# Side stages' matmuls ranked first in the planner, and three operands moved to other byte offsets

## The chip, the cores and the metric

One core of one Trainium2 chip runs the kernel. TensorE (PE for its matmuls, PEld for its weight loads), VectorE (DVE), ScalarE (ACT) and GpSimd (POOL) work side by side; transfers are issued from the SP queue. The metric is the device time in microseconds of one execution. The kernel before took 2572.21 us, the median of three runs (2569.39 to 2573.22). Outside the profile's span lie some 2 us of each execution.

## The reference

For x of shape 8 x 3008 x 256 the reference takes the real FFT along the sequence, multiplies every frequency by a complex 256 x 256 matrix and adds a complex bias, shrinks real and imaginary part towards zero by 0.01, and transforms back. The result, as 24064 rows of 256, goes through a feed-forward layer.

```python
X = np.fft.rfft(x, axis=1)
Yr = Xr @ w_r - Xi @ w_i + b_r
Yi = Xr @ w_i + Xi @ w_r + b_i
Yr, Yi = soft_threshold(Yr, 0.01), soft_threshold(Yi, 0.01)
y = np.fft.irfft(Yr + 1j * Yi, n=3008, axis=1)
h = y @ w_in                      # 256 -> 2048
out = (h * np.clip(h + 3, 0, 6) / 6) @ w_out    # 2048 -> 256
```

## The kernel before

The feed-forward layer is the bulk. It is cut into 47 chunks of 512 rows and 8 bands of the hidden width, 376 units. A unit goes through four phases of `w_in` matmuls (`phase_a` to `phase_d`, a Strassen form with seven block products), a gate on ScalarE and VectorE (`gate`), and four steps of `w_out` matmuls (`down`). Every operand here is a pair of fp32r numbers, high and low, and a product is three matmuls: low x high, high x low, high x high (`product`, line 137; `down`, line 651). All of these matmuls have 256 columns. Stationary operands are `w_in` and `w_out`, moving ones `yb` and `gs`.

The Fourier transforms are the side stages, one batch after the other, and all but the first batch run between the feed-forward units:

- `stage1` (line 268): 47-point transforms over blocks of 120 rows. For batches 2 to 7, and most of batch 1, it splits the data into `xs` (high, low) and calls `product`, three matmuls of 512 columns (256 for the last block), with the constant `f47` stationary and `xs` moving.
- `middle` (line 366) for each of 12 groups of two frequencies: `s2` (line 390), four fp32 matmuls of 128 columns on the loaded tile `bt`; `s3`, 18 matmuls of 256 columns with the weights `w_r`, `w_m`, `w_i` moving; `s4`, which splits `zt` into `z`; `s5` (line 465), a `product` of three matmuls of 512 columns with the constant `g64` stationary and `z` moving.
- `segment` (line 485): 47-point transforms back, seven segments in a batch; for each half `dh` four fp32 matmuls of 120 columns (two of 96 in the last segment) on the loaded tile `qt`, whose results go into the chunks `raw` of the feed-forward layer. `qt` has one buffer, `bt` two.

An fp32 matmul stands in the trace as two records, an fp32r one as one.

All side stages put their results into PSUM tiles called `ps_a`, of which there are two (`room`); in the stages of batch 0 some go to `pb`. Their tiles are handed out in program order.

The order on each engine is made by a planner when the kernel is built: it plays the program against durations that it assumes, and on every engine it takes, of the instructions whose inputs it believes ready, the one of the best rank. The rank is the position in the program, unless an instruction stands under `tc.high_priority()`: that one comes ahead of all others. Before the change this holds for the copies and additions that empty the feed-forward PSUM tiles (`kept`, `added`), and for no matmul. The program puts the pieces of the side stages into slots between the units' phases (`lay`, `slots`, `fill`). On the chip each engine keeps the planner's order, and an instruction whose input is not there holds up all behind it.

SBUF is laid out by hand, through the order in which tiles are made and through small filler tiles. Tiles with the same `tag` share a place. With the bytes of each tile added up, the starts modulo 256 are: `w_in` and `w_out` 160, `X` 160, `z` and `xs` 160, `f47` 192 (high) and 128 (low), `g64` 96, `yb`, `gs`, `bt`, `qt` and the weights `w_r`, `w_m`, `w_i` 96. A filler `gap` of 192 bytes behind `X` turns 160 into 96.

```python
home = ("a", "h", "z", "h", "xs", "h", "X")[q % 7] if b == 0 else ("a", "ot", "ot")[q % 3] if b == 1 and whole else "a"
a = space([P, 2 * D], F32, "a", home)[:rows, :w]
if home == "X":
    space([P, 48], F32, "gap")
```

In batch 0 `stage1` borrows places for its results `a` by these tags; the order in which the tags first occur is the order of the places.

Of the kernel before, what the change touches and what calls it, by code (L numbers as in the profile page):

```python
# [23 lines left out]
NK = N2 // 2 + 1  # L24
# [76 lines left out]
def spectral_ffn(ctx: ExitStack, tc: tile.TileContext, x, w_r, w_i, bias, w_in, w_out, f47, f64, g64, sgn, out):  # L101
# [31 lines left out]
    def product(ps, terms, start=True, stop=True, more=False):  # L133

        todo = [p for (ah, al), (bh, bl) in terms for p in ((al, bh), (ah, bl), (ah, bh))]
        for n, (a, b) in enumerate(todo):
            nc.tensor.matmul(  # L137
                out=ps,
                lhsT=a,
                rhs=b,  # L140
                start=start and n == 0,
                stop=stop and n == len(todo) - 1,
                skip_group_check=more,
            )
# [122 lines left out]
    split(*f47_s)  # L267


    scr1, scr2, stores = {}, {}, []  # L270

    def stage1(b):
        scr1[b] = dram.tile([2, N1, NK, D], F32, name="scr1")
        sets = SEGS[-1:] + SEGS[:-1]
        xins = {}

        def load(i):
            n1, n = sets[i]
            rows, w = (R47, 2 * D) if n == 2 * J else (n * NK, D)
            if b == 0:  # L280
                xins[i] = spare[i]
            elif b == 1 and i < 4:
                if i % 2 == 0:
                    xins[i], xins[i + 1] = twin([P, 2, 2 * D], F32, "xin", "gs")
            else:
                xins[i] = space([P, 2, 2 * D], F32, "xin")
            at = n1 // J * 2 * D
            src = x[b, :rows, at : at + 2 * w].rearrange("p (s c) -> p s c", s=2)
            nc.sync.dma_start(out=xins[i][:rows, :, :w], in_=src)
            return rows, w  # L290

        shapes = [load(i) for i in range((len(sets), 4, 1)[min(b, 2)])]
        for i, (n1, n) in enumerate(sets):
            rows, w = shapes[i]
            xin = xins.pop(i)
            plus, minus = xin[:rows, 0, :w], xin[:rows, 1, :w]
            whole = b == 0 or b == 1 and i < 4
            e = space([P, 2 * D], F32, "e", "r" if whole else "e")[:rows, :w]
            on = nc.vector if whole else nc.gpsimd
            on.tensor_tensor(out=e, in0=plus, in1=minus, op=ALU.add)  # L300
            on.tensor_tensor(out=plus, in0=plus, in1=minus, op=ALU.subtract)
            for c, src in enumerate((e, plus)):
                q = 2 * i + c
                if whole:
                    ps = room(c == 1)
                    turns = f47_s[2][:rows, c * R47 : c * R47 + rows]
                    nc.tensor.matmul(out=ps[:rows, :w], lhsT=turns, rhs=src, start=True, stop=True)
                else:
                    xs = [t[:rows, :w] for t in twin([P, 2 * D], F32R, "xs")]
                    split(*xs, src, nc.gpsimd)  # L310
                    yield
                    ps = room()
                    product(ps[:rows, :w], [([t[:rows, c * R47 : c * R47 + rows] for t in f47_s[:2]], xs)])
                home = ("a", "h", "z", "h", "xs", "h", "X")[q % 7] if b == 0 else ("a", "ot", "ot")[q % 3] if b == 1 and whole else "a"
                a = space([P, 2 * D], F32, "a", home)[:rows, :w]
                if home == "X":
                    space([P, 48], F32, "gap")
                nc.scalar.copy(out=a, in_=ps[:rows, :w])
                dst = scr1[b][c, n1 : n1 + n].rearrange("(g j) k d -> (j k) g d", g=w // D)
                stores.append(nc.sync.dma_start(out=dst, in_=a.rearrange("p (g d) -> p g d", d=D)))  # L320
                if c and i + 1 < len(sets) and i + 1 >= len(shapes) and not whole:
                    shapes.append(load(i + 1))
                yield
            if whole and i + 1 == len(shapes) and i + 1 < len(sets):
                shapes.append(load(i + 1))

    bias_s = const.tile([P, 2 * D], F32, name="bias")
    sgn_s = const.tile([P, NK], F32, name="sgn")
    w_m = [const.tile([P, 2 * D], F32R, name="w_m_" + t) for t in ("hi", "lo")]
    w_four = []  # L330

# [18 lines left out]
        yield  # L350

    run(stage1(0))
    with tc.issue_after(stores[-1].ins):
        r, k = [loaded(w, P, 2 * D, n, t) for w, n, t in ((w_r, "w_r", spare[7]), (w_i, "w_i", spare[8]))]
        nc.sync.dma_start(out=bias_s, in_=bias)
        g64_t = loaded(g64, P, P, "g64")
        nc.sync.dma_start(out=sgn_s, in_=sgn)
        const.tile([P, 16], F32, name="last")
    w_four += [twin([P, 2 * D], F32R, "w", tag) for tag in ("T", "qt")]
# [11 lines left out]
    def middle(b):  # L371
# [16 lines left out]
        def s2(g):  # L388
            data, f = bt.pop(g)
            ps = room(b == 0)  # L390
            psv = ps.rearrange("p (h r k c) -> p h r k c", h=2, r=2, k=2)
            for u in range(2):
                for dh in range(2):
                    nc.tensor.matmul(  # L394
                        out=psv[:, dh, :, u, :],
                        lhsT=data[:, u, dh * P : (dh + 1) * P],
                        rhs=f[:, u, :],
                        start=True,
                        stop=True,
                    )  # L400
            if g + 2 < NG:
                load(g + 2)
            pv = ps.rearrange("p (h r c) -> p h r c", h=2, r=2)
            hi, lo = twin([P, 2, 3, P], F32R, "X", tag(g, "X", "gs", "gs"))
            if b:
                xi = space([P, 2, P], F32, "xi")
                nc.scalar.copy(out=xi, in_=pv[:, :, 1])
            split(hi[:, :, :2], lo[:, :, :2], pv)
            if b:
                nc.vector.tensor_tensor(out=xi, in0=pv[:, :, 0], in1=xi, op=ALU.add)  # L410
                split(hi[:, :, 2], lo[:, :, 2], xi)
            xs[g] = (hi, lo)
# [52 lines left out]
        def s5(g):  # L465
            ps = room(b == 0)
            flat = lambda t: t.rearrange("p k d -> p (k d)")
            if b:
                product(ps, [(g64_s, [flat(t) for t in zs.pop(g)])])
            else:  # L470
                nc.tensor.matmul(out=ps, lhsT=g64_t[2], rhs=flat(zs.pop(g)), start=True, stop=True)
            pt = space([P, 2, D], F32, "pt", tag(g, "pt", "ot", "ot"))
            nc.scalar.copy(out=pt, in_=ps.rearrange("p (k d) -> p k d", d=D))
            nc.sync.dma_start(out=dst[:, 2 * g : 2 * g + 2, :], in_=pt)
# [20 lines left out]
    def segment(b, k, tag="qt", aside=None):  # L495
# [22 lines left out]

        for dh in range(2):
            ps = room(bool(aside) and dh == 1)  # L520
            for cs in range(2):
                for g in range(gr):
                    nc.tensor.matmul(  # L523
                        out=ps[:, cs * w + g * rows : cs * w + (g + 1) * rows],
                        lhsT=qt[:rows, cs, g, dh * P : (dh + 1) * P],
                        rhs=f47_s[2][:rows, cs * R47 : cs * R47 + rows],
                        start=True,
                        stop=True,
                    )
            odd = space([P, 2 * R47], F32, "odd", aside or "xi")[:, :w]  # L530
            nc.scalar.copy(out=odd, in_=ps[:, w : 2 * w])
            for c, q, lo, hi in places(0, w):
                nc.vector.tensor_tensor(out=raw[c][:, dh, q : q + hi - lo], in0=ps[:, lo:hi], in1=odd[:, lo:hi], op=ALU.add)

            some = lambda a: a.rearrange("p (n q) -> p n q", q=NK)[:, :, 1:]
            m = NK - 1
            for c, q, lo, hi in places(w, n * m):
                while lo < hi:
                    row, col = divmod(lo, m)
                    if col == 0 and hi - lo >= m:  # L540
                        r1, c1 = hi // m, m
                    else:
                        r1, c1 = row + 1, min(m, col + hi - lo)
                    size = (r1 - row) * (c1 - col)
                    nc.vector.tensor_tensor(
                        out=raw[c][:, dh, q : q + size].rearrange("p (n q) -> p n q", n=r1 - row),
                        in0=some(ps[:, :w])[:, row:r1, col:c1],
                        in1=some(odd)[:, row:r1, col:c1],
                        op=ALU.subtract,
                    )  # L550
                    lo, q = lo + size, q + size
            yield
# [260 lines left out]
```

## Time and profile before

| | |
|---|---|
| median of 3 runs | 2572.21 us |
| the profiled execution itself | 2572.28 us |
| its span, first to last instruction | 2570.1 us |
| PE busy | 2509.0 us, 98% of the span, 20910 records |
| PEld busy | 2449.8 us, 95% |
| DVE busy | 1969.8 us, 77% |
| ACT busy | 1823.2 us, 71% |
| POOL busy | 773.6 us, 30% |
| chain that ended last, PE's share | 89% |

A matmul's record lasts longer than the time until the next one starts, since matmuls are pipelined. So the busy time of PE says only that it is never empty; its pace is read from the starts. In the timeline view neighbours of one line and tile are merged into one row with their count, and the start of the next row less the start of this one, over the count, is the pace. The view by form gives the mean length of a record, which grows with the pace.

### The profile page before, as it was taken

The page shows a single profiled execution, that of the slowest core. Times are in us where ns is not written, and L with a number is a line of the kernel's source. Part 1 is how long each engine was busy: PE and PEld are TensorE (multiplying, and loading weights), DVE is VectorE, ACT ScalarE, POOL GpSimd, SP SyncE. Part 2 cuts the span into 40 slices and gives each one's busy share as a digit, 9 for nine tenths or more (in the row PEclk, how much of TensorE's full clock was granted, in tenths as well). Part 3 has the DMA queues.
Part 4 walks back from the last instruction along what each step waited for, and adds up shares of the span by engine and source line. Part 5 has one row for each costly group of instructions (what it writes and reads, how often), then busy time and mean ns, then how long its engine had stood idle before and what let it go on. Part 6 is the DMA issues. An engine that isn't in the chain of part 4 may idle for free.

```text
span 2570.1 us, 53411 instructions
## 1 busy us (share of the span) xinstructions
PE 2509.0 (98%) x20910; PEld 2449.8 (95%) x20910; DVE 1969.8 (77%) x3189; ACT 1823.2 (71%) x3584; POOL 773.6 (30%) x738
## 2 busy tenths in 40 slices
PE   6789999999999999999999999999999999999999
PEld 4579999999999999999999999999999999999998
DVE  7778878877787777778777777877778777767766
ACT  6477777777777777777777677767776777766676
POOL 3353442333233332333313343234321221121310
PEclk8889999999999999999999999999999999999999
DMA  8633432332133222232223222222222121110000
GB/s 245 193 114 104 131 97 83 90 91 71 58 94 87 65 71 71 80 91 72 76 73 89 66 78 84 75 78 81 71 74 60 52 66 51 37 37 21 12 18 17
DMA packets 150115, 200.54 MB, mean 78 GB/s; under 512 B 16847, under 2 KB 103943, under 8 KB 149863
## 3 DMA queue, kind: packets, MB, share of 16 engines
q1 hardware_dynamic: 149863, 197.13, 26.6%
q8 instruction: 164, 2.69, 0.5%
q14 instruction: 88, 0.72, 0.1%
HBM read 97.45 MB, written 74.97 MB: 67 GB/s over the span
## 4 chain that ended last, share of the span: by engine, by line
PE 89%; DVE 4%; DMA 3%; ACT 2%; issue 1%; SPq 1%; POOL 0%; ACTq 0%; DVEq 0%; POOLq 0%
PE po L651 38%; PE pb L137 19%; PE ps_a L137 11%; PE pc L137 9%; PE pd L137 5%; PE ps_a L523 3%; PE ps_a L394 3%; ACT gs L130 1%; DVE r L628 1%; DMA scr<-a 1%; ACT r L626 1%; DMA zt<-tc 1%; DMA x_lo<-in_x 0%; DMA bt<-scr 0%; DVE h L590 0%
## 5 line engine op out<-in xcount | busy, mean ns | idle before, releaser
L651 PE MATMUL po<-gs,w_out_hi 128*128 128x256 f32 x6016 | 1029.4, 277 | 0.0
L651 PEld LDWEIGHTS po<-gs,w_out_hi 128*128 128x128 f32 x6016 | 843.0, 188 | 1.6
L628 DVE SCALAR_TENSOR_TENSOR r<-r,h 128x1024 f32<-128x1024 f32 x376 | 479.9, 1276 | 270.0 <-ACT r L626 268.7
L651 PE MATMUL po<-gs,w_out_lo 128*128 128x256 f32 x3008 | 605.6, 279 | 2.2 <-ACT gs L130 1.1
L626 ACT ACTIVATE r<-h,three 128x1024 f32<-128x1024 f32 x376 | 434.5, 1156 | 217.3 <-DVE h L590 215.9
L137 PE MATMUL pb<-yb,w_in_hi 128*128 128x256 f32 x3008 | 570.7, 278 | 1.1 <-DVE yb L131 1.1
L131 DVE TENSOR_TENSOR gs<-r,gs 128x1024 fp32r<-128x1024 f32 x376 | 483.3, 1285 | 100.1 <-ACT gs L130 97.4
L130 ACT CAST gs<-r 128x1024 fp32r<-128x1024 f32 x376 | 395.3, 1051 | 110.7 <-DVE r L628 108.0
L651 PEld LDWEIGHTS po<-gs,w_out_lo 128*128 128x128 f32 x3008 | 461.1, 188 | 8.3 <-ACT gs L130 6.1
L137 PEld LDWEIGHTS pb<-yb,w_in_hi 128*128 128x128 f32 x3008 | 458.3, 189 | 4.6 <-DVE yb L131 1.3
L131 POOL TENSOR_TENSOR yb<-T,yb 128x256 fp32r<-128x256 f32 x184 | 172.2, 938 | 875.2 <-ACT yb L130 859.6
L137 PE MATMUL pb<-yb,w_in_lo 128*128 128x256 f32 x1504 | 427.7, 287 | 2.6 <-ACT yb L130 1.2
L590 DVE TENSOR_TENSOR h<-pc,u 128x256 f32<-128x256 f32 x752 | 314.9, 419 | 101.2 <-PE pc L137 93.0
L585 ACT COPY u<-pb 128x256 f32<-128x256 f32 x752 | 278.9, 373 | 110.4 <-PE pb L137 101.7
L137 PE MATMUL pc<-yb,w_in_hi 128*128 128x256 f32 x1504 | 296.2, 278 | 0.6 <-DVE yb L131 0.6
L137 PEld LDWEIGHTS pb<-yb,w_in_lo 128*128 128x128 f32 x1504 | 282.9, 189 | 7.7 <-ACT yb L130 1.4
L137 PEld LDWEIGHTS pc<-yb,w_in_hi 128*128 128x128 f32 x1504 | 228.9, 189 | 1.7 <-DVE yb L131 0.9
L137 PE MATMUL pc<-yb,w_in_lo 128*128 128x256 f32 x752 | 212.9, 283 | 1.3 <-DVE h L590 1.2
L585 ACT COPY p<-pb 128x256 f32<-128x256 f32 x376 | 139.3, 371 | 53.8 <-PE pb L137 51.3
L619 ACT COPY h<-pb 128x256 f32<-128x256 f32 x376 | 140.9, 375 | 39.2 <-PE pb L137 37.7
L590 DVE TENSOR_TENSOR h<-pd,p 128x256 f32<-128x256 f32 x376 | 156.8, 417 | 9.4 <-ACT p L585 6.8
L131 POOL TENSOR_TENSOR xs<-xin,xs 120x512 fp32r<-120x512 f32 (+1 forms) x45 | 58.7, 1304 | 321.1 <-ACT xs L130 307.8
(139 smaller groups left out, 3989.0 us busy)
## 6 DMA issues: line engine op xcount, KB each, us to landing
bt<-scr SPq DMA_DIRECT2D x96, 256.0 KB, 3.0
scr<-pt SPq DMA_DIRECT2D x96, 256.0 KB, 2.3
zt<-tc SPq DMA_DIRECT2D x376, 64.0 KB, 2.0
out<-ot SPq DMA_DIRECT2D x94, 256.0 KB, 2.3
scr<-a SPq DMA_DIRECT2D x96, 240.0 KB, 2.6
qt<-scr SPq DMA_DIRECT2D x96, 240.0 KB, 3.5
xin<-in_x SPq DMA_DIRECT2D x42, 480.0 KB, 4.5
f<-in_f SPq DMA_DIRECT2D x96, 128.0 KB, 2.9
```

The lines of the kernel that those rows point to most:

```text
L130: nc.scalar.copy(out=hi, in_=src)
L131: (on or nc.vector).tensor_tensor(out=lo, in0=src, in1=hi.bitcast(F32), op=ALU.subtract)
L137: nc.tensor.matmul(out=ps, lhsT=a, rhs=b, start=start and n == 0, stop=stop and n == len(todo) - 1, skip_group_check=more,)
L394: nc.tensor.matmul(out=psv[:, dh, :, u, :], lhsT=data[:, u, dh * P : (dh + 1) * P], rhs=f[:, u, :], start=True, stop=True,)
L523: nc.tensor.matmul(out=ps[:, cs * w + g * rows : cs * w + (g + 1) * rows], lhsT=qt[:rows, cs, g, dh * P : (dh + 1) * P], rhs=f47_s[2][:row ...
L585: nc.scalar.copy(out=t, in_=ps)
L590: nc.vector.tensor_tensor(out=to, in0=ps, in1=keep.pop((i, n)), op=ALU.add)
L619: nc.scalar.copy(out=hs[i][:, 1, :H], in_=pb)
L626: nc.scalar.activation(out=r, in_=h, func=AF.Relu, bias=three, scale=1.0)
L628: nc.vector.scalar_tensor_tensor(out=r, in0=r, scalar=6.0, in1=h, op0=ALU.min, op1=ALU.mult)
L651: nc.tensor.matmul(out=pos[dh][:, cols], lhsT=w[:, ft * D + dh * P : ft * D + (dh + 1) * P], rhs=g[:, low, u, cols], start=f == 0 and u == ...
```

## The change

Four places put their matmuls under `tc.high_priority()`: the `xs` product of `stage1`, `s2`, the `z` product of `s5` for batches 1 to 7, and `segment`. `s3`, and the operations on other engines, keep their rank. The other edits move bytes: in batch 0 `stage1` borrows the places `T` and `zt` where it borrowed `z` and `xs`, so that `T` and `zt` lie ahead of the filler `gap` (at 160) and `z` and `xs` behind it (at 96); `g64` is made ahead of the weights, at 32; `sgn` is put into the filler `gap`, and small fillers keep all else where it was.

```diff
-    scr1, scr2, stores = {}, {}, []
+    scr1, scr2, stores, signs = {}, {}, [], []
...
                     ps = room()
-                    product(ps[:rows, :w], [([t[:rows, c * R47 : c * R47 + rows] for t in f47_s[:2]], xs)])
-                home = ("a", "h", "z", "h", "xs", "h", "X")[q % 7] if b == 0 else ("a", "ot", "ot")[q % 3] if b == 1 and whole else "a"
+                    with tc.high_priority():
+                        product(ps[:rows, :w], [([t[:rows, c * R47 : c * R47 + rows] for t in f47_s[:2]], xs)])
+                home = ("a", "h", "T", "h", "zt", "h", "X")[q % 7] if b == 0 else ("a", "ot", "ot")[q % 3] if b == 1 and whole else "a"
                 if home == "X":
-                    space([P, 48], F32, "gap")
+                    signs.append(space([P, 48], F32, "gap")[:, :NK])
...
-    sgn_s = const.tile([P, NK], F32, name="sgn")
+    const.tile([P, 8], F32, name="rest")
+    g64_t = [const.tile([P, P], dt, name="g64_" + t) for t, dt in (("hi", F32R), ("lo", F32R), ("all", F32))]
+    const.tile([P, 16], F32, name="next")
...
+    sgn_s = signs[0]
...
-        g64_t = loaded(g64, P, P, "g64")
+        nc.sync.dma_start(out=g64_t[2], in_=g64)
...
         def s2(g):
-            for u in range(2):
-                for dh in range(2):
-                    nc.tensor.matmul(
...
+            with tc.high_priority():
+                for u in range(2):
+                    for dh in range(2):
+                        nc.tensor.matmul(
...
         def s5(g):
             if b:
-                product(ps, [(g64_s, [flat(t) for t in zs.pop(g)])])
+                with tc.high_priority():
+                    product(ps, [(g64_s, [flat(t) for t in zs.pop(g)])])
...
     def segment(b, k, tag="qt", aside=None):
-            for cs in range(2):
-                for g in range(gr):
-                    nc.tensor.matmul(
...
+            with tc.high_priority():
+                for cs in range(2):
+                    for g in range(gr):
+                        nc.tensor.matmul(
```

## Rows read from the trace of the kernel before

**Rows 1.** Windows: stretch, its us, busy us (records) PE PEld DVE ACT POOL, clock, DMA share, GB/s

```profile
0.00:200.00 200.00, 150.30 (x880) 120.97 (x880) 148.93 (x258) 121.65 (x238) 78.20 (x81) 0.87 0.61 180
200.00:2390.00 2190.00, 2184.57 (x18558) 2157.01 (x18558) 1700.16 (x2754) 1582.92 (x3129) 665.02 (x627) 1.00 0.26 74
2390.00:2570.00 180.00, 174.15 (x1477) 171.85 (x1475) 120.73 (x179) 118.62 (x218) 30.43 (x30) 1.00 0.05 17
```

**Rows 2.** Lines by form, PE alone, 200 to 2390 us: busy, mean ns, idle before

```profile
L137 PE MATMUL pb<-yb,w_in_hi 128*128 128x256 f32 x2690 | 510.0, 277 | 0.0
...
L523 PE MATMUL ps_a<-f_all,qt 120*128 120x120 f32 x692 | 98.7, 274 | 0.4 <-DMA qt<-scr 0.4
...
L394 PE MATMUL ps_a<-f,bt 128*128 128x128 f32 x664 | 94.1, 274 | 0.3 <-DMA bt<-scr 0.3
...
L137 PE MATMUL ps_a<-z,g_hi 128*128 128x512 f32 x168 | 52.9, 393 | 0.0
...
L137 PE MATMUL ps_a<-xs,f_hi 120*120 120x512 f32 x144 | 45.8, 392 | 0.0
L137 PE MATMUL ps_a<-z,g_lo 128*128 128x512 f32 x84 | 34.1, 406 | 0.5 <-DVE raw L545 0.5
L137 PE MATMUL ps_a<-xs,f_lo 120*120 120x512 f32 x72 | 29.5, 409 | 0.0
L523 PE MATMUL ps_a<-f_all,qt 96*128 96x96 f32 x56 | 8.5, 266 | 0.0
L137 PE MATMUL ps_a<-xs,f_hi 96*96 96x256 f32 x24 | 5.0, 281 | 0.0
```

**Rows 3.** Timeline of PE, feed-forward matmuls alone: start us, length us, what, count

```profile
1185.71 0.39 PE L651 MATMUL po<-gs,w_out_lo 128*128 128x256 f32 x2
1185.94 0.96 PE L651 MATMUL po<-gs,w_out_hi 128*128 128x256 f32 x7
1186.73 0.28 PE L137 MATMUL pb<-yb,w_in_lo 128*128 128x256 f32 x1
```

**Rows 4.** Timeline of PE around one s2 group, 1526 to 1531 us

```profile
1526.67 0.39 PE L394 MATMUL ps_a<-f,bt 128*128 128x128 f32 x2
...
1527.61 0.60 PE L394 MATMUL ps_a<-f,bt 128*128 128x128 f32 x4
...
1528.40 0.38 PE L394 MATMUL ps_a<-f,bt 128*128 128x128 f32 x2
...
1529.10 0.40 PE L651 MATMUL po<-gs,w_out_lo 128*128 128x256 f32 x2
...
1530.04 0.28 PE L137 MATMUL pb<-yb,w_in_lo 128*128 128x256 f32 x1
```

**Rows 5.** Timeline of PE around another s2 group, 1239 to 1241 us

```profile
1239.29 1.05 PE L394 MATMUL ps_a<-f,bt 128*128 128x128 f32 x8
...
1240.42 0.28 PE L137 MATMUL pb<-yb,w_in_lo 128*128 128x256 f32 x1
...
1240.99 0.39 PE L651 MATMUL po<-gs,w_out_lo 128*128 128x256 f32 x2
```

**Rows 6.** Timeline of PE: two short pieces of side groups, at 379 and 2267 us

```profile
379.44 0.38 PE L394 MATMUL ps_a<-f,bt 128*128 128x128 f32 x2
...
2267.84 0.38 PE L523 MATMUL ps_a<-f_all,qt 120*128 120x120 f32 x2
```

**Rows 7.** Timeline of PE around one z group, 1181 to 1184 us

```profile
1181.94 0.39 PE L137 MATMUL ps_a<-z,g_lo 128*128 128x512 f32 x1
1182.17 0.62 PE L137 MATMUL ps_a<-z,g_hi 128*128 128x512 f32 x2
1182.63 0.28 PE L137 MATMUL ps_a<-w_r_hi,X 128*128 128x256 f32 x1
...
1183.34 0.28 PE L137 MATMUL pb<-yb,w_in_lo 128*128 128x256 f32 x1
```

**Rows 8.** Waits, the whole span: who for whom, us in total, times, longest us

```profile
PEld po L651 <- ACT gs L130: 6.1, 20, 0.9
```

More of the change, by code (lines that the diff above doesn't have):

```diff
@@ L391, in s2 @@
             psv = ps.rearrange("p (h r k c) -> p h r k c", h=2, r=2, k=2)
-            for u in range(2):
-                for dh in range(2):
-                    nc.tensor.matmul(
[L395 to L400, printed above, removed]
+            with tc.high_priority():
+                for u in range(2):
+                    for dh in range(2):
+                        nc.tensor.matmul(
+                            out=psv[:, dh, :, u, :],
+                            lhsT=data[:, u, dh * P : (dh + 1) * P],
+                            rhs=f[:, u, :],
+                            start=True,
+                            stop=True,
+                        )
             if g + 2 < NG:
@@ L520, in segment @@
             ps = room(bool(aside) and dh == 1)
-            for cs in range(2):
-                for g in range(gr):
-                    nc.tensor.matmul(
[L524 to L529, printed above, removed]
+            with tc.high_priority():
+                for cs in range(2):
+                    for g in range(gr):
+                        nc.tensor.matmul(
+                            out=ps[:, cs * w + g * rows : cs * w + (g + 1) * rows],
+                            lhsT=qt[:rows, cs, g, dh * P : (dh + 1) * P],
+                            rhs=f47_s[2][:rows, cs * R47 : cs * R47 + rows],
+                            start=True,
+                            stop=True,
+                        )
             odd = space([P, 2 * R47], F32, "odd", aside or "xi")[:, :w]
```

## The prediction

> **What bounds the kernel.** I read the windows first. From 200 to 2390 us PE is busy 2184.6 of 2190 us at a clock of 1.00 (the level of 2.4 GHz), while VectorE works 1700 us and ScalarE 1583 [rows 1]. Only the first 200 us (150.3 busy, clock 0.87) and the last 180 (174.2) leave PE idle for longer. So the long middle is a queue of matmuls, and what counts there is the pace at which they start. That comes from starts in the timeline: 9 feed-forward matmuls from 1185.71 to 1186.73 give 1.02 / 9 = 113.3 ns each [rows 3]. No stretch of matmuls of 256 columns goes faster, so this is the floor.
>
> **What the middle loses against that floor.** It holds 18,558 records [rows 1]. 692 + 664 + 56 = 1412 are fp32 records, 168 + 144 + 84 + 72 = 468 have 512 columns [rows 2], and the other 16,678 have 256. At 113.3 ns for 256 columns, twice that for 512, and 111.7 for an fp32 record (the pace inside an unbroken run), that is 1890 + 106 + 158 = 2154 us; 36 us are lost. I take them apart by the timeline:
>
> - A slow pace. After the pieces in [rows 4] four matmuls from 1529.10 on would take 0.453 us at the floor; the eight from 1529.10 to 1530.04 take 0.94 us, 117.5 each. Such a pace lasts until the next side group, then is gone or not. 2368 matmuls of the middle run at 116 to 120 ns, mean 117.7: 2368 x 4.4 = 10.4 us.
> - fp32 runs. A whole s2 group, from 1239.29 to the third fp32r matmul at 1240.42, takes 1.13 us, less two matmuls 0.90 [rows 5]. The group in [rows 4] is cut into 2 + 4 + 2 records; its last two take 1529.10 - 1528.40 less four matmuls = 0.25 us, its four (1527.61 to 1528.40, with three fp32r matmuls) 0.79 - 0.34 = 0.45. With the first two taken like the last, 0.25 + 0.45 + 0.25 = 0.95, or some 20 ns for each cut; two halves of four come to 14. There are 268 runs in the stretch for 184 groups.
> - The z and xs groups. From 1181.94 to 1183.34 run three matmuls of 512 and six of 256 columns: 1.40 us, where the floor is 12 x 0.1133 = 1.36 [rows 7]. The median over all of them is 34 ns a group, in 84 z and 84 xs groups (those of 256 columns too): 5.7 us.
> - Waits. What remains is 36 - 10.4 - 268 x 14 ns - 5.7 = 16 us, mostly for the gate's `gs` [rows 8] and for `yb`; DMAs ended only 0.4 and 0.3 us of them at side groups [rows 2].
>
> **The ranking.** It adds and removes no instruction and no DMA. Today a side matmul ranks by its place in the program, so a feed-forward matmul of an earlier place that the planner believes ready halfway through takes the next turn, and the group falls into pieces. Ranked first, a group once begun is run to its end. Two terms follow.
>
> What a piece does to the pace: I sorted every side run between 200 and 2390 us by whether the stretch behind it is slow. Behind 187 unbroken groups 690 of 7822 matmuls are slow (12 runs start a slow stretch). Behind 107 pieces, of which the first and the last with a slow stretch stand in [rows 6], it is 1502 of 3556 (27 runs). Behind the other 123 runs (halves of four, neighbours run together) it is 176 of 3678. If all pieces behaved as whole groups, 3556 x 0.088 = 313 would be slow in place of 1502: 1189 x 4.4 ns = 5.2 us. The bounds are 0 (the pace is set by something that goes with pieces) and 10.4 (no slow stretch is left).
>
> What a cut costs itself: 268 - 184 = 84 cuts at 14 to 20 ns, taken at 17: 1.4 us.
>
> What moves with it: side tiles in `ps_a` are handed out in program order from two buffers, so a group can overtake feed-forward matmuls, but no side group; the 18 matmuls of `s3` keep their low rank and stay as filler for holes. Behind a side group on PE's queue stands the feed-forward work, which then comes at most one group (0.9 us) later, and its next user is a gate several phases away. I take the waits as unchanged at 16 us, with bounds of -5 and +15 (a third gone, or doubled).
>
> **The bytes.** In the feed-forward product the moving operand starts at 96 and the stationary one at 160 modulo 256. The z and xs products move from 160. That the offset matters I read from a form with the same number of columns: `xs` at 256 columns lasts 281 ns, `pb` from `yb` 277 [rows 2], and the length of a record grows with the pace. After the change both move from 96 as the feed-forward does, and the last matmul of a group meets the next weights (160) in the pair that runs at the floor. Inside the groups the pairs 96 with 32 (z) and 96 with 192 (xs, first half) occur nowhere here; the nearest rows are 0 extra (feed-forward) and the 34 ns of today. Most of the 34 lies in the five matmuls behind the group, so I take three quarters: 168 x 25 ns = 4.3 us, bounds 0 and 5.7, and 5.7 lost if the new pairs are as much worse.
>
> The Trainium skill, "SBUF — State Buffer", section "SBUF: two separate sides", says that TensorE's ports never wait on anyone; by it no offset would matter and this term were 0. The row of 281 against 277 speaks against that, though with 24 records only.
>
> `T`, which holds weights of batch 0, moves from 96 to 160: 72 matmuls at 4 ns more, 0.3 us lost. `g64`, `sgn` and the fillers issue the same DMAs in the same order, in a stretch where PE is idle for 50 of 200 us [rows 1]; that idle time hides it. The ranking of `s2` and `segment` there may shift the start by some us either way; I take 0, and 5 us (a tenth of the idle time) as bound on both sides.
>
> **Sum.** 5.2 + 1.4 + 4.3 - 0.3 = 10.6 us. The profiled execution took 2572.28 us (span 2570.1), practically the median of 2572.21. Forecast: 2561.7 us.
>
> **Rivals.**
> - *The offsets do nothing.* 10.6 - 4.3 = 6.3 gained: 2566.0 us. For it: the 34 ns may be the price of changing the number of columns. Against it: the 256-column form above. The sentence of the Trainium skill on ports would give this too.
> - *Groups stay broken, or pieces are not the cause.* A group's matmuls could become ready one by one, so that rank doesn't bind them; or the slow pace returns after any run. Only the offsets remain: 2572.3 - 4.0 = 2568.3. Against it: all matmuls of a group read the same tiles; and 27 of 107 against 12 of 187.
> - *The waits eat it.* Side work spread between units fills the holes in which `gs` or `yb` is late. Put in lumps as early as it can, it leaves the holes open: the waits go from 16 to 26 us, 2572. For it: in the last 180 us, with hardly any side work, 5.9 us of PE are idle [rows 1], thirteen times the middle's rate (5.4 in 2190).
> - *PE stalls on side inputs (slower).* The planner puts a ranked group where it believes the input lands. PE keeps that order, so where the transfer is later on the chip all 113-ns matmuls behind it stand still. Today such groups come late enough: 0.7 us of waits in all for `qt` and `bt` [rows 2]. 54 segments with one `qt` buffer and 83 s2 groups make 137 loads; at the 0.35 us that the two waits last on average, 30 late loads use up the gain, and 45 make it slower by more than 0.2%. With half of them late: 68 x 0.35 - 10.6 = +13, 2585 us. Against it: `bt` is loaded two groups ahead, and the two PSUM buffers, not the loads, will mostly be last.
>
> **How the numbers follow.** 0.2%, 5.1 us, is about what a measurement of this kernel can tell from no change. Chances: forecast 0.52, offsets do nothing 0.14, groups stay broken 0.08, waits eat it 0.12, stalls on side inputs 0.14. Faster than 2567.1: nearly all of the first, most of the second, a third of the third: 0.63. Slower than 2577.3: the last and a little of the fourth: 0.16. The rest, 0.21, is within. The range reaches down by the bounds of pace and start (5.2 + 3 more: 2553) and up over the third and fourth cases to 2576; the last rival and the far ends of the others stay outside. The forecast's own range is 2553 to 2568.
>
> **What would show it.** Right: in the timeline of the middle all L394 rows come as x8 (or more) and L523 as x8 or x4; stretches of 117.7 ns become rare; the starts after a z group are at 113 ns at once; the mean length of `z,g_hi` falls from 393 towards 390 and of `xs` (256 columns) from 281 to 277; PE's records in the middle are as many, in some 10 us less. Wrong: waits of PE at L394 or L523 on DMA of more than some us in all, or on `gs` of over 10 us; x2 rows of L394 still there; or whole groups followed by the slow pace as often as pieces are now. Any of these makes the forecast wrong in its own term; a start of the first feed-forward unit that is later by over 5 us would make it wrong in all.

## The result and the profile after

The changed kernel takes 2586.02 us (median of 6 runs, 2584.69 to 2589.85), the kernel before 2572.72 us on the same chip (6 runs): ratio 1.0055, interval 1.0045 to 1.0065. It is slower by 13.3 us. The forecast was 2561.7 us, the range 2553 to 2576: wrong in sign, and outside the range. The profiled execution took 2586.86 us (span 2585.1), 14.6 more than that of before.

The windows of the changed kernel, with the columns of [rows 1]:

```profile
0.00:200.00 200.00, 149.38 (x849) 119.49 (x850) 145.85 (x249) 117.33 (x231) 76.94 (x79) 0.86 0.61 180
200.00:2390.00 2190.00, 2178.09 (x18461) 2145.87 (x18460) 1684.61 (x2746) 1565.14 (x3112) 667.01 (x622) 1.00 0.26 74
2390.00:2585.00 195.00, 189.14 (x1605) 186.82 (x1604) 131.26 (x195) 132.20 (x243) 38.87 (x38) 1.00 0.04 16
```

PE's idle time in the middle went from 5.4 [rows 1] to 11.9 us, and it ran 97 records fewer there. So the loss is spread over the middle, and part of it is PE standing still, in a stretch where it stood still for only 0.25% of the time before. From 200 to 2545 us, the stretch of the sums below, the kernel before and the changed one have

```profile
200.00:2545.00 2345.00, 2339.35 (x19875) 2310.49 (x19875) 1807.73 (x2915) 1689.46 (x3329) 695.45 (x657) 1.00 0.24 70
...
200.00:2545.00 2345.00, 2332.72 (x19778) 2299.00 (x19777) 1792.08 (x2909) 1674.74 (x3318) 705.88 (x660) 1.00 0.24 70
```

that is 5.7 and 12.3 us of idle time.

Lines by form, PE alone, 200 to 2390 us, to be laid beside [rows 2]:

```profile
L530 PE MATMUL ps_a<-f_all,qt 120*128 120x120 f32 x696 | 92.0, 274 | 0.7 <-DMA qt<-scr 0.7
L399 PE MATMUL ps_a<-f,bt 128*128 128x128 f32 x664 | 87.8, 274 | 0.1
...
L137 PE MATMUL ps_a<-z,g_hi 128*128 128x512 f32 x168 | 53.0, 395 | 0.0
...
L137 PE MATMUL ps_a<-z,g_lo 128*128 128x512 f32 x84 | 33.3, 396 | 0.2 <-DVE raw L552 0.2
...
L137 PE MATMUL ps_a<-xs,f_hi 96*96 96x256 f32 x24 | 4.8, 281 | 0.0
```

The busy time of `bt` and `qt` fell by 6.3 and 6.7 us at nearly equal counts and equal mean length, because runs overlap more when they are whole. The lengths that the offsets were to shorten did not fall: `z,g_hi` 395 ns (393 before), `xs` at 256 columns 281 as before; only `z,g_lo` did (396 after 406). DMAs end 0.7 us at `qt` and nothing at `bt`: side inputs are not late for PE.

Waits over the whole span of the changed kernel (who for whom, us, times, longest us):

```profile
ACT z L130 <- DMA zt<-tc: 30.8, 28, 2.9
...
ACT xs L130 <- POOL e L300: 19.0, 9, 4.1
...
PEld po L658 <- ACT gs L130: 15.0, 37, 2.9
...
PE po L658 <- ACT gs L130: 5.6, 5, 2.7
```

and two of them in the kernel before, whose third row stands in [rows 8]:

```profile
ACT z L130 <- DMA zt<-tc: 13.2, 16, 2.6
...
ACT xs L130 <- POOL e L300: 4.6, 5, 1.4
```

The gate's casts (`gs`) now hold PE's weight loads up for 15.0 us instead of 6.1, and ScalarE stands 30.8 us at transfers of `zt` and 19.0 at GpSimd's `e`, instead of 13.2 and 4.6. The costliest of these stops, in the timeline of all engines of the changed kernel:

```profile
1160.12 0.28 PE L137 MATMUL ps_a<-w_r_hi,X 128*128 128x256 f32 x1
1160.23 1.26 POOL L300 TENSOR_TENSOR e<-xin 120x512 f32<-120x512 f32 x1 [8.05 <-DMA xin<-in_x]
1161.52 0.62 ACT L130 CAST xs<-e 120x512 fp32r<-120x512 f32 x1 [3.66 <-POOL e L300]
...
1162.04 1.04 ACT L130 CAST gs<-r 128x1024 fp32r<-128x1024 f32 x1
...
1163.14 0.71 PE L658 MATMUL po<-gs,w_out_lo 128*128 128x256 f32 x2 [2.74 <-ACT gs L130]
```

GpSimd waits 8.05 us for `xin`; ScalarE, which takes its instructions in order, waits 3.66 us for GpSimd's `e` with the cast of `gs` behind it; PE runs out of work after 1160.12 and stands 2.74 us until that cast is done. It is the longest of PE's stops in that stretch, and it has a second price. The windows of the same kernel around it:

```profile
1160.00:1163.00 3.00, 0.39 (x4) 0.20 (x2) 0.00 (x0) 1.48 (x3) 2.69 (x3) 1.00 0.04 14
1163.00:1165.00 2.00, 1.86 (x9) 1.87 (x10) 1.89 (x1) 0.89 (x4) 1.06 (x1) 0.56 0.00 0
1165.00:1167.00 2.00, 2.00 (x12) 2.00 (x12) 1.93 (x7) 0.00 (x0) 0.00 (x0) 0.58 0.00 0
1167.00:1169.00 2.00, 2.00 (x20) 2.00 (x19) 0.45 (x1) 1.69 (x3) 0.00 (x0) 1.00 0.00 0
```

After the stop the granted clock is 0.56 and 0.58 for some 4 us (near the level of 1.2 GHz) and 1.00 again from 1167 on. Those two windows hold 21 matmuls, where the next one alone holds 20. At 214 ns from start to start in place of 113 the 15 matmuls of that time cost 1.5 us. Between 200 and 2545 us it is the only stretch of the changed kernel with a lower clock; the kernel before has none there.

**Where the 14.6 us went.** For every matmul of both traces I took the time to the next start, less 113.3 ns per 256 columns (fp32 records: 107 ns per 128 columns, a base somewhat below the prediction's 111.7), and sorted what is over, from 200 to 2545 us:

```
                          before   after   difference
late starts, longer         15.2    25.3     +10.1
starts some 220 ns apart     4.0     8.0      +4.0
slow pace (117.7 ns)        13.7    12.4      -1.2
fp32 runs and 2 after       17.2    16.2      -1.0
z and xs groups              5.6     4.8      -0.8
lost in the first 200 us    78.2    81.6      +3.4
                                             +14.5
```

The first two rows are PE's waits, and they hold more than its idle time: a matmul that starts late by less than the length of a record leaves no idle time behind. The second row is such starts, nearly all of them single. One in the kernel before, in the timeline of all engines:

```profile
700.95 1.05 ACT L130 CAST gs<-r 128x1024 fp32r<-128x1024 f32 x1
701.04 0.28 PE L137 MATMUL pb<-yb,w_in_lo 128*128 128x256 f32 x1
...
702.05 0.30 PEld L651 LDWEIGHTS po<-gs,w_out_lo 128*128 128x128 f32 x2
702.06 0.49 PE L651 MATMUL po<-gs,w_out_lo 128*128 128x256 f32 x2
...
702.39 0.40 PE L651 MATMUL po<-gs,w_out_hi 128*128 128x256 f32 x2
...
703.33 0.40 PE L651 MATMUL po<-gs,w_out_hi 128*128 128x256 f32 x2
```

The cast of `gs` ends at 702.00, the first weight load for a matmul on `gs` starts at 702.05, and the two matmuls from 702.06 take 0.33 us in place of 0.23. The clock is 1.00 there, as in all of this kernel from 200 to 2545 us; of the 8.0 us of the changed kernel only the 1.5 behind the stop at 1160 are at the lower clock. The pace changes with the wait too: the nine matmuls from 701.04 take 113.3 ns each, the eight from 702.39 take 117.5.

By what PE waited for, the first two rows together (19.2 to 33.3) are `gs` 6.9 to 18.0, `yb` 6.6 to 9.6, all else 5.7 as before. What the change was to save it saves in small (3.0 us); the waits and the start take 17.5.

### The profile page after: what moved, and what is told of

The parts are those of the page before. It is cut to its first block, busy times and chain, and to the rows that moved or that the text cites. A ratio compares the mean times of both kernels' runs of the same rounds, so it can differ in the third digit from the quotient of the medians.

```text
span 2585.1 us, 53382 instructions
## 1 busy us (share of the span) xinstructions
PE 2516.6 (97%) x20910; PEld 2452.2 (95%) x20910; DVE 1961.7 (76%) x3189; ACT 1814.7 (70%) x3584; POOL 782.8 (30%) x738
## 4 chain that ended last, share of the span: by engine, by line
PE 86%; ACT 3%; DVE 3%; DMA 3%; issue 1%; POOL 1%; SPq 0%; ACTq 0%; DVEq 0%; POOLq 0%
PE po L658 37%; PE pb L137 18%; PE ps_a L137 11%; PE pc L137 9%; PE pd L137 4%; PE ps_a L530 3%; PE ps_a L399 3%; ACT gs L130 1%; DMA xin<-in_x 1%; DMA zt<-tc 1%; ACT r L633 1%; DVE r L635 1%; DMA scr<-pt 0%; ACT yb L130 0%; POOL e L300 0%
## 5 line engine op out<-in xcount | busy, mean ns | idle before, releaser
L131 DVE TENSOR_TENSOR gs<-r,gs 128x1024 fp32r<-128x1024 f32 x376 | 489.7, 1302 | 100.7 <-ACT gs L130 97.1
L137 PE MATMUL pb<-yb,w_in_lo 128*128 128x256 f32 x1504 | 421.9, 283 | 4.0 <-ACT u L592 3.0
L137 PE MATMUL pd<-yb,w_in_hi 128*128 128x256 f32 x752 | 149.2, 278 | 1.2 <-DVE yb L131 1.2
```

Of the source, the lines that this page charges most:

```text
L131: (on or nc.vector).tensor_tensor(out=lo, in0=src, in1=hi.bitcast(F32), op=ALU.subtract)
L137: nc.tensor.matmul(out=ps, lhsT=a, rhs=b, start=start and n == 0, stop=stop and n == len(todo) - 1, skip_group_check=more,)
```

## The experiments

Thirteen kernels, five rounds each. The runs of the kernel before that share their chip have medians of 2570.92 (first four kernels), 2572.55 (next four), 2571.5 (three) and 2571.8 us (the last two). "PE waits" below are the first two rows of the table together, 200 to 2545 us; cuts are places in the program's PE order at which a side group is interrupted (before 125, changed kernel 34; in the traces, where one shows only as a change to another kind of matmul, I count 123 and 18, and 8 for the 12 of `glue_old` below).

**1. The two halves of the change.** Only the byte offsets (every `tc.high_priority()` of the change taken out):

```diff
-                    with tc.high_priority():
-                        product(ps[:rows, :w], ...)
+                    product(ps[:rows, :w], ...)
```

> New byte offsets alone, no ranking: the order of the matmuls is that of before. Theory E (the ranking costs, by putting side groups early and leaving the feed-forward's holes open): nothing of the cost is here, 2571 to 2573 us; z groups 13 ns cheaper, 84 x 13 = 1.1 us. Theory O (the offsets cost: a z or xs group at 160 put a slow stretch back to 113 ns, at 96 it leaves it slow or starts one): slow matmuls behind z and xs groups rise from some 300 to over 1000, +3 us or more, 2575 to 2577.

Measured: 2573.93 us, ratio 1.0015 (1.0006 to 1.0024). The order of PE's instructions is that of before. PE waits 17.8 us, but 4055 matmuls at the slow pace instead of 3013, 18.2 us instead of 13.7. The offsets cost time instead of gaining 4.3 us. The time lies between the ranges of the two theories; the count of slow matmuls is that of theory O.

Only the ranking (`z`, `xs`, `T`, `g64` and `sgn` where they were):

```diff
-                home = ("a", "h", "T", "h", "zt", "h", "X")[q % 7] if b == 0 else ...
+                home = ("a", "h", "z", "h", "xs", "h", "X")[q % 7] if b == 0 else ...
```

> Ranking alone, z, xs and g64 where they were. Theory E: waits of PE in the middle stay at 33 us and the start stays 3.4 us late, 2584 to 2587. Theory O: the slow pace falls to 4 us or less behind whole groups (12 now), so at most 2578 if the offsets are the larger part of the loss; with both, 2578 to 2583.

Measured: 2583.25 us, ratio 1.0048 (1.0035 to 1.0060). 34 cuts, PE waits 32.2 us, slow pace 9.9 us, 82.6 us lost by 200 us. So the ranking carries nearly all of the loss, and its own saving (slow pace 13.7 to 9.9) is there too.

**2. Whole, but not early.** The first matmul of a side group keeps the rank of its place; only those behind it are ranked first, so that a group is not interrupted, but begins where it did:

```diff
+    def behind(first):
+        return tc.high_priority() if first else nullcontext()
...
+            with behind(glued and n):          # product: n is the matmul's number
+                    with behind(u or dh):      # s2
+                    with behind(cs or g):      # segment
```

With the old offsets:

> Old offsets; the first matmul of a side group keeps the rank of its place, only the others come first, so that a group begun is run to its end but not begun earlier. Theory E (being early costs, not being whole): waits back at 16 to 20 us, start as before, cuts 125 to 12, slow pace under 6 us: 2562 to 2568. Rival L (the lump of 0.9 us ahead of the feed-forward costs): waits stay at 30 us or more, 2580 or above.

Measured: 2562.84 us, ratio 0.9971 (0.9959 to 0.9984). 12 cuts, PE waits 18.0 us, slow pace 6.8 us. It beats both kernels.

With the new offsets:

> As glue_old, with the new offsets. Theory E alone: 1 us below glue_old (z groups 13 ns cheaper). Theory O: 3 to 6 us above glue_old, since more stretches behind z and xs groups run at 117.7 ns.

Measured: 2569.27 us, ratio 0.9990 (0.9981 to 0.9999). PE waits 18.0 us, 2249 slow matmuls for 1479. The same offsets take 6.4 us here, 3.5 of them in the slow pace and 1.9 in the first 200 us. Wholeness gains, with PE's waits unchanged.

**3. Earliness alone.** As `glue_old`, with the first matmul of each group ranked a little ahead of its place:

```diff
-        return tc.high_priority() if first else nullcontext()
+        return tc.high_priority() if rest else tc.high_priority(offset=100)
...
-            with behind(glued and n):
+            with behind(n) if glued else nullcontext():
```

> glue_old, with the first matmul of each side group ranked 100 places of the program earlier (some five phases, 6 us of PE), the others first as in glue_old. Theory E (earliness leaves the feed-forward's holes open): waits of PE in the middle between glue_old's 18.0 and rank_old's 32.2 us, 22 to 28, and 2566 to 2575 us. Rival A (only the absolute first rank, over every other instruction, hurts): as glue_old, 2561 to 2565.

Measured: 2578.73 us, ratio 1.0029 (1.0018 to 1.0041). 16 cuts, PE waits 29.6 us. Both are above what theory E had here (2566 to 2575 us, 22 to 28).

And a little behind its place (`offset=-100`):

> glue_old, with the first matmul of each side group ranked 100 places later. Theory E: the groups fill more holes, waits 12 to 18 us, at most 2563 us, unless the side stages now end late for the chunks that need them; in that case waits for raw or yb rise and it is slower than glue_old. Rival A: as glue_old.

Measured: 2567.36 us, ratio 0.9982 (0.9973 to 0.9991). 11 cuts, PE waits 19.5 us, slow pace 8.9 us. Three kernels with whole groups that differ in one number: early 2578.73, at their place 2562.84, late 2567.36 (the first and the last on another chip than the second; as ratios 1.0029, 0.9971 and 0.9982, and the intervals of the last two overlap). Over the whole span the waits that go with it are, in the kernel with early groups,

```profile
ACT z L130 <- DMA zt<-tc: 20.2, 19, 3.4
...
PEld po L657 <- ACT gs L130: 8.7, 23, 1.8
...
PEld pb L141 <- ACT h L625: 3.7, 5, 2.0
```

and in that with groups at their place

```profile
ACT z L130 <- DMA zt<-tc: 11.3, 18, 1.4
...
PEld po L657 <- ACT gs L130: 6.2, 16, 1.1
...
PEld pb L141 <- ACT h L625: 0.8, 3, 0.3
```

The larger part of the rise is not at `gs` here: sorted by the operand that PE's late matmul works on, `gs` rises by some 4.5 us and `yb` by some 6.2, mostly in waits for the copies and additions that empty the feed-forward PSUM tiles (`h`, `u`). What holds those up was not separated.

**4. Which groups must not be early.** `s2` and `segment` ranked first from their first matmul on, `z` and `xs` only from their second:

```diff
-                    with behind(u or dh):
+                    with behind(True):
-                    with behind(cs or g):
+                    with behind(True):
```

> Old offsets; s2 and segment ranked first whole, z and xs only from the second matmul on. 204 of the 366 groups behind the first 200 us are ranked early, with 169 of 267 us of side work other than s3. Theory E: waits 24 to 30 us, 2570 to 2580; if the loss is one of place and not of share, all of rank_old's 12 us are here.

Measured: 2577.46 us, ratio 1.0022 (1.0012 to 1.0033). 38 cuts, PE waits 28.4 us, 82.9 us lost by 200 us. As with `early100`, more of the rise is at `yb` (some 6.7 us) than at `gs` (3.9).

The other way round:

```diff
-            with behind(glued and n):
+            with behind(glued):
```

> Old offsets; z and xs ranked first whole, s2 and segment only from the second matmul on. Here first-ranked z and xs cut fp32 groups (125 cuts in all, as many as before, for 12 in glue_old), some 1.5 us of that. Theory E: waits 20 to 26 us, 2566 to 2575. The first 200 us hold few z and xs, so the later start (3.4 us) should be absent here and present in rank_fp32.

Measured: 2573.49 us, ratio 1.0010 (1.0001 to 1.0019). Inconclusive: 125 cuts are left, 38 of them in `z` groups and 38 in `s2` groups, so the groups are no longer whole. PE's idle time from 200 to 2545 us is 9.3 us, against 5.5 in `glue_old`, which speaks for waits from early `z` and `xs` groups as well. Being early costs for the fp32 groups without the others: 2577.46 against 2562.84.

**5. Which offset.** `glue_old` with only `xs` at 96, only `z` at 96, and `z` at 96 with `g64` at 32 (the layout of the change for `g64` and `sgn`). In all three `T` moves to 160.

```diff
-                home = ("a", "h", "z", "h", "xs", "h", "X")[q % 7] if b == 0 else ...
+                home = ("a", "h", "z", "h", "T", "h", "X")[q % 7] if b == 0 else ...     # xs96
+                home = ("a", "h", "xs", "h", "T", "h", "X")[q % 7] if b == 0 else ...    # z96
```

> glue_old with xs alone at 96 (z at 160, g64 at 96); T goes to 160 with it. Theory O: xs groups now start slow stretches where they started none (behind xs groups from a fast stretch 5 of 38 in offs, 0 of 40 in before), some 30 stretches less what fp32 and z groups end: 2 to 4 us above glue_old. Rival: the harm sits in z alone, then as glue_old.

> glue_old with z alone at 96 (xs at 160, g64 at 96). Theory O: a z group that arrives slow stays slow (11 of 13 in offs, 0 of 9 in before) but starts none, so slow stretches get longer: 1 to 3 us above glue_old. Rival: z at 96 with g64 at 96 (the same offset for both operands) is dearer inside the group, over 34 ns.

> As z96 with g64 at 32: tells the stationary operand's offset from the moving one's. Theory O: as z96 within 1 us, z groups at 20 ns over the floor in place of 33.

Measured: 2564.85 us, ratio 0.9974 (0.9965 to 0.9983); 2564.46 us, 0.9973 (0.9961 to 0.9984); 2565.47 us, 0.9977 (0.9968 to 0.9986). None differs from `glue_old` (0.9971) by more than the intervals, though all stand on the slower side. The time does not tell which offset costs; the pace behind the groups does, below. Inside a `z` group it is `z` itself and not `g64`: the median over the floor is 21 ns with `z` at 96 whether `g64` lies at 96 or at 32, and 34 with `z` at 160, so the expectation that only `g64` at 32 would lower it was wrong.

**6. Is it ScalarE standing at late inputs?** The casts `z<-zt` and `xs` (from `e` and from `xin`) moved from ScalarE to GpSimd, which forms the low halves of `xs` anyway; those of `z` go there too:

```diff
-        nc.scalar.copy(out=hi, in_=src)
+        if alone:
+            on.tensor_copy(out=hi, in_=src)
+        else:
+            nc.scalar.copy(out=hi, in_=src)
...
-                    split(*xs, src, nc.gpsimd)
+                    split(*xs, src, nc.gpsimd, True)
...
-            split(*zs[g], zt)
+            split(*zs[g], zt, nc.gpsimd, True)
```

With the ranking and the old offsets:

> The ranking of the changed kernel with the old offsets, and the casts z<-zt and xs<-e moved from ScalarE to GpSimd, which already forms their low halves. ScalarE then no longer stands in front of a late transfer with the gate's casts behind it, while side work is still as early as in rank_old (2583.25 us, PE waits 32 us after 200 us, 20.4 us above glue_old). Theory A, ScalarE standing at transfers makes the waits: PE waits fall to about 20 us, the time to some 2571, and the distance to glue_pool is 10 us or less. Theory B, holes that are left without side work make them: waits stay at 28 us or more, the time at 2578 or more, and the distance to glue_pool is 15 us or more. In between: both have a part.

Measured: 2571.66 us, ratio 1.0006 (0.9995 to 1.0017).

As control, with `glue_old`:

> glue_old (2562.84 us, PE waits 18 us) with the same casts moved to GpSimd: what the move does by itself. ScalarE stands for 11 us at zt and 8 at e there, and little of that reaches PE. Both theories: within 5 us of glue_old. Below 2558 us would show that these stands cost PE time without the ranking too; above 2568 that GpSimd's slower cast makes z or xs late.

Measured: 2561.82 us, ratio 0.9965 (0.9953 to 0.9977), from `glue_old` not to be told apart.

The distance between early and not early fell from 20.4 (2583.25 - 2562.84) to 9.8 us. That is the number of theory A, but its reason holds only in part. In the waits of `rank_old` over the whole span

```profile
ACT z L130 <- DMA zt<-tc: 27.9, 29, 3.0
...
PEld po L655 <- ACT gs L130: 13.1, 36, 2.2
```

and of `rank_pool`, from 200 to 2545 us,

```profile
PEld po L658 <- ACT gs L133: 5.8, 22, 0.3
...
PEld pd L140 <- DVE h L597: 4.1, 4, 2.7
...
PEld ps_a L399 <- DVE raw L552: 2.4, 1, 2.4
...
PEld ps_a L530 <- DMA qt<-scr: 2.1, 1, 2.1
```

the gate's casts hold PE up far less: in both rows of the table together PE's waits for `gs` fall from 16.1 to 9.8 us (6.2 in `glue_old`), and no single stand of the weight loads is over 0.3 us. So of the 9.9 us that the ranking adds at `gs`, 6.3 go with the side casts on ScalarE. The move takes the casts' own time off ScalarE as well as its stands; in the control it changed little (weight loads wait 4.7 us for `gs` in `glue_old` and 4.2 in `glue_pool`, 200 to 2545 us), which speaks for the stands. But all PE waits fell only from 32.2 to 29.9 us, not to 20: three or four long stops at other places took their room (2.7 us behind `h`, 2.4 at an `s2` group, 2.1 at `qt`). The larger part of the 11.6 us came from the slow pace, 9.9 to 3.2 us, and the first 200 us, 82.6 to 77.7, which no theory had named.

## Why the prediction was wrong

**"I take the waits as unchanged."** This is the step that failed, and it alone turns the sign: +14.1 us, at the edge of its own upper bound of +15. The text looked for the damage behind the side group on PE's queue and found little. It lies on ScalarE's: a side group issued early asks earlier for `z` and `xs`, whose casts stand on ScalarE in order ahead of the gate's, and where the transfer or GpSimd's `e` is late the gate stands too. Experiments 2 and 3 show that earliness makes the waits (18.0, 29.6 and 32.2 us with nearly all groups whole each time), experiment 6 that the side casts on ScalarE carry 6 of the 10 us at `gs`. The rest of the way from earliness to waits, at `gs` and, in the kernels with early fp32 groups, at `yb`, stays open. That the holes also lack side work to fill them, the reason of the rival, is argued from one count only: in the 3 us before a wait for `gs` side matmuls are 3 to 7% of PE's time, against 20% on the whole. It was not tried by itself.

**"I take 0" for the start** was +3.4 us, within its bound of 5. The kernels with `s2` and `segment` ranked first lose 81.6, 82.6 and 82.9 us there, but 77.7 with the casts on GpSimd; all others lie between 76.5 and 81.1. What sets it was not separated.

**The offsets, "4.3 us, bounds 0 and 5.7, and 5.7 lost if the new pairs are as much worse".** The third end came true in size. Moving them costs 3.0 us alone and 6.4 with whole groups; in the slow pace it is 4.5 and 3.5 us, and 2.5 between `rank_old` and the changed kernel. The term itself, the 34 ns of a `z` group, did fall (median 33 to 20 ns), but for `xs` it did not (34 to 33), 0.8 us in all. What was missed is what a group does to the pace of the hundreds of matmuls behind it. The offsets alone cost time, 1.0015 (1.0006 to 1.0024), with 1042 more slow matmuls at an unchanged order. The Trainium skill, "SBUF — State Buffer", section "SBUF: two separate sides", says that TensorE never waits on anyone at its ports. It says so of waiting on other engines, and no run here shows what happens at the ports; the prediction's step from there to offsets that cost nothing does not agree with these runs.

**The slow pace, "313 would be slow in place of 1502 ... 5.2 us".** The reasoning holds, where the offsets leave it alone. Behind whole groups of `rank_old` 1245 of 13,545 matmuls are slow, 9.2%, for the 8.8% assumed, and the term is 3.7 us (13.7 to 9.9); in `glue_old` 7.8% and 6.9 us. In the changed kernel it is 1864 of 13,545, 13.8%, and 1.2 us are left. The text had a slow pace last until the next side group; the rows at 702 us show that a wait can start it as well, so that more waits also work against this term.

**The cuts, 84 at 17 ns = 1.4 us.** Right in kind: fp32 runs fell from 268 to 193, and 75 cuts gave 1.0 us, 14 ns each. A whole `s2` group of the changed kernel, in the timeline of PE,

```profile
1518.87 1.05 PE L399 MATMUL ps_a<-f,bt 128*128 128x128 f32 x8
...
1519.68 0.37 PE L137 MATMUL pb<-yb,w_in_lo 128*128 128x256 f32 x1
...
1519.89 0.28 PE L137 MATMUL pb<-yb,w_in_hi 128*128 128x256 f32 x1
...
1520.01 0.40 PE L137 MATMUL ps_a<-z,g_lo 128*128 128x512 f32 x1
```

takes 1.14 us to its third follower, less two matmuls 0.91, as in [rows 5] (0.90).

**The rivals.** "The waits eat it" had the place right, PE's waits at `gs` and `yb`, and the size wrong: 26 us in place of 33. Its evidence was misread: of the 5.9 us that PE is idle in the last 180 us, 5.6 lie behind 2545, where the program ends, and from 2390 to 2545 it is 0.23 of 155 us, less than the middle's rate. Starts some 220 ns apart are denser there (0.8 us in 100, against 0.2 in the middle), so the reason is not refuted either. "PE stalls on side inputs" gave the right time, 2585, for a wrong reason: `qt` and `bt` rose from 1.3 to 1.7 us of PE waits; the inputs that are late are `zt` and `xin`, and PE meets them through ScalarE. "Groups stay broken" fell with 125 cuts to 34. "The offsets do nothing" fell on its other side.

The chance of slower, 0.16, was put almost whole on one mechanism, transfers that are late for PE; the doubled waits, which the text had as a bound, had hardly a chance beyond the break-even.

## What the offsets do

The same `z` group with the same matmuls ahead of and behind it, in the kernel before (`z` at 160), timeline of PE:

```profile
2128.18 0.64 PE L651 MATMUL po<-gs,w_out_hi 128*128 128x256 f32 x4
2128.65 0.40 PE L137 MATMUL ps_a<-z,g_lo 128*128 128x512 f32 x1
2128.88 0.63 PE L137 MATMUL ps_a<-z,g_hi 128*128 128x512 f32 x2
...
2131.39 0.39 PE L651 MATMUL po<-gs,w_out_lo 128*128 128x256 f32 x2
...
2132.98 0.28 PE L137 MATMUL pb<-yb,w_in_lo 128*128 128x256 f32 x1
```

and with only the offsets moved (`z` at 96):

```profile
2130.24 0.63 PE L654 MATMUL po<-gs,w_out_hi 128*128 128x256 f32 x4
2130.72 0.40 PE L137 MATMUL ps_a<-z,g_lo 128*128 128x512 f32 x1
2130.95 0.63 PE L137 MATMUL ps_a<-z,g_hi 128*128 128x512 f32 x2
...
2133.54 0.40 PE L654 MATMUL po<-gs,w_out_lo 128*128 128x256 f32 x2
...
2135.19 0.28 PE L137 MATMUL pb<-yb,w_in_lo 128*128 128x256 f32 x1
```

Both are in the slow pace ahead of the group: the four `po` matmuls take 0.47 and 0.48 us, where the fast pace needs 0.45. From the first of the 14 `po` matmuls behind it to the next `pb` the first takes 1.59 / 14 = 113.6 ns each, the second 1.65 / 14 = 117.9. The group at 160 has reset the pace, the group at 96 has not. Counted over the middle, for groups with a stretch of some length on both sides:

```
                        slow stretch ahead, fast behind   fast ahead, slow behind
before        z 160          9 of 9                          1 of 38
              xs 160         7 of 7                          0 of 40
glue_old      z 160          7 of 7                          1 of 50
              xs 160         9 of 9                          0 of 48
offs          z 96           2 of 13                         -
              xs 96          6 of 9                          5 of 38
changed       z 96           2 of 8                          5 of 59
              xs 96          -                              10 of 60
xs96          z 160         16 of 16                         -
              xs 96          -                               5 of 48
z96_g32       z 96           1 of 7                          -
              xs 160        11 of 11                         -
z96 (g64 96)  z 96           6 of 8                          -
```

A dash stands where no count was made. So the price of a pair of offsets is not in the group. At 160 whole groups ended every slow stretch that they met in these counts, and the change took that away for `z` and in part for `xs`: a count of mine with other limits for the stretches gives 58 of 58 for the seven other kernels with both at 160, and in the changed kernel 0 of 5 for `z` and 9 of 13 for `xs`. The place of `g64` seems to bear on it too: with `z` at 96, 6 of 8 beside `g64` at 96, 1 of 7 beside `g64` at 32, which are few. The single moves of experiment 5 show the same states, but too few of them to be seen in the time. Side groups are not alone in this: in stretches without any `z`, `xs` or fp32 group a count of mine finds 17 changes of pace in the kernel before and 20 in the changed one, each at a late start. What sets the two paces stays open.

## What to carry to other kernels

To keep a group of matmuls together, rank only its second and later ones: the first then still waits for its turn, and work that fills holes stays late (0.9971 here, where ranking whole groups gave 1.0048). Before a side group is moved earlier, follow its inputs back through every engine that takes instructions in order, and look at what stands behind the late instruction there. A wait costs more than the idle time that the profile shows: here 12.3 us idle were 33.3 us of late starts. A change that makes one operation match its neighbours has to be judged by the stretch behind it, not by the operation's own length.

## What the runs showed of the hardware

- PE runs matmuls of 256 columns at one of two steady paces, 113.3 or 117.7 ns, and keeps one of them for up to some hundred matmuls until a side group or a wait changes it (702 us above); the granted clock is 1.00 at both. `z` and `xs` groups, whose moving operand starts at 160 modulo 256, ended the slow one each time (32 of 32 in the kernel before and `glue_old`), groups at 96 seldom or in part.
- A stop of PE of 2.7 us was followed by some 4 us at a granted clock of 0.56 to 0.58, with matmuls 214 ns apart (1163.64 to 1165.35, eight matmuls), which cost 1.5 us. Not every stop was: behind one of 2.2 us at an `s2` group in `rank_pool` the clock is 1.00 (1228 to 1232 us).
- A matmul whose weight load starts together with it, and not some 0.1 us ahead, is followed late, here 0.33 us for two matmuls in place of 0.23 at a clock of 1.00, and the profile counts no idle time for it.
